# Transposing transfers from tile 12 on instead of tile 15, 12 load buffers instead of 18, and another place for the loads in the queue

## The chip, the cores and the metric

The kernel runs on one core of one Trainium2 chip. The metric is the time of one execution on the device, in microseconds (us); lower is better. The engines that matter are TensorE (PE, matrix products and transposes), VectorE (DVE), ScalarE (ACT), GpSimd (POOL, which here mostly issues loads) and SyncE (SP, which here issues transfers). Each of them works through its own instructions strictly in the order in which the program was written, and waits on semaphores where an operand isn't there.

## The reference

Chunked attention with memory slots, followed by a gated feed-forward network over all tokens. `q`, `k` and `v` are 4 batches x 8 heads x 768 positions x 64; each batch and head has 8 memory keys and values.

```python
chunk, left_ctx, right_ctx = (32, 16, 8)
for c in range(S // chunk):
    l_start, r_end = max(0, c*chunk - left_ctx), min(S, (c+1)*chunk + right_ctx)
    k_full = concat([mem_k, k[:, :, l_start:r_end]]); v_full = concat([mem_v, v[:, :, l_start:r_end]])
    a = softmax(scale * q_c @ k_full.T)
    out[:, :, c*chunk:(c+1)*chunk] = a @ v_full
x = out.transpose(0, 2, 1, 3).reshape(3072, 512)
return (relu(x @ w_gate) * (x @ w_val)) @ w_out        # 512 -> 1536 -> 512
```

## The kernel before

**Tiles and blocks.** The 3072 tokens are 24 tiles of 128 tokens, six to a batch: tiles 0 to 5 are batch 0, 6 to 11 batch 1, 12 to 17 batch 2, 18 to 23 batch 3. Attention is done tile by tile. The feed-forward network is done in eight blocks of `BLOCKS = [2, 2, 2, 4, 4, 4, 4, 2]` tiles, so block 3 holds tiles 6 to 9, block 4 tiles 10 to 13, block 5 tiles 14 to 17, block 6 tiles 18 to 21 and block 7 the last two. A block runs `first` (L407, products with `w_gate` and `w_val` into `g_ps` and `v_ps`, then ReLU on ACT, L413, and the gating product on DVE, L419) and then `second` (L432, the product with `w_out` into `out_ps`, copied and stored).

**One tile's attention**, with the keys of the operations in the program's own list of them (`ops`), `a` the tile and `i` 0 for q and 1 for k:

- `("qk", a, i)`: POOL loads q or k of the tile into a buffer of `ldpool` (L254), cast to bf16. There are 18 such buffers; the six v tiles of batch 0 come first and use them too.
- `("t", a, i)`, `("tc", a, i)`: the tile is transposed. For tiles 6 to 14 PE does it with four transposes into PSUM (L275), and ACT or DVE copies the result into `qT` or `kT`. For tiles from `LATE_QK` = 15 on, SP issues a transposing transfer from SBUF to SBUF (L283): q goes straight into `qT`, k into a buffer `k_t` (three of them) that ACT or DVE copies into `kT`. (Batch 0 has a way of its own, L236.)
- `("s", a)`: 32 small products give the scores (L309). Those of a tile also need the k of the next tile of its batch.
- `max`, `sub`, `exp`, `sum`, `rec`, `nrm`: the softmax, five operations on DVE (L322 to L352) and the exponent on ACT. Its result is `p_n`.
- `("p", a)`, `("pc", a)`: the probabilities P are transposed into `pT`, with four transposes on PE (L358) and a copy, or from tile `LATE_P` = 15 on by a transposing transfer of SP (L362).
- `("v", a)`: the value products (L388; L381 in batch 0) with `v_bd`, and `("x", a)`: the copy into `xT`, which the block's `first` reads.

`v_bd` has two copies: `v_bd[0]` serves batches 0 and 2, `v_bd[1]` batches 1 and 3. For batches 1 to 3, POOL loads v into it (`("vl", b, n)` and `("ve", b, n)`, L185, four issues), copies the memory rows into it (`("mr", b, n)`, L168, eight issues; for batch 1 SP does that), and ACT or DVE copies rows up inside it (`("up", ...)`). Batch 2's load waits until `v_bd[0]` has been zeroed after tile 5's values; batch 3's waits for tile 11's values.

**The order of the work** is written out ahead by a planner, `schedule()`. It has a list of operations with an assumed duration, dependencies (each with an assumed delay, where a number stands beside it), a priority and buffers to take and give (`room`), and steps through time: whenever an engine is free, it gets the ready operation of the best priority. Attention goes before feed-forward products, which fill the rest. The planner's times are assumptions only; what stays of them in the program is the order on each engine, and on the chip the semaphores decide. Of the constants: `ISSUE` is SP's time for one transposing transfer, `LAND` and `LAND_P` the time from there until its result is taken as there (q and k; P), `MARGIN` = 1.0 is added for attention products on PE. `pace(a)` holds PE's transposes of a tile back until a mark in the feed-forward work, `LEAD` = 31 us of it ahead of the block's start and 5.2 us later for each further tile; `pace_t(a)` holds SP's transfers of q and k back until the scores of an earlier tile have been put in the order. POOL's loads go in the order in which they were listed: `late` lists q and k of tiles 6 to 23, two a tile, k first; its first five stand ahead of `w_out`, and the loop over the batches lists each batch's v and memory rows and then a slice of `late`.

Of the kernel before, what the change touches and what calls it, by code (L numbers as in the profile page):

```python
# [19 lines left out]
def kernel(  # L20
# [24 lines left out]
    NT = B * TPB  # L45
# [7 lines left out]
    BAND0 = 48  # L53
    UT = 3

    LATE_QK, LATE_P = 15, 15

    KEY_RUNS = ((0, CH, 0), (KW, 64, CH), (CH, KW, CTX))
    assert sum(BLOCKS) == NT and NMEM == 8 and D == 64 and H == 8

    const = ctx.enter_context(tc.tile_pool(name="const", bufs=1))
    ldpool = ctx.enter_context(tc.tile_pool(name="ldpool", bufs=18))
    kvpool = ctx.enter_context(tc.tile_pool(name="kvpool", bufs=2))
    smpool = ctx.enter_context(tc.tile_pool(name="smpool", bufs=2))
    xtpool = ctx.enter_context(tc.tile_pool(name="xtpool", bufs=2))
# [294 lines left out]
    def p_transfer(a):  # L360
        PT[a] = smpool.tile([128, HP, 128], F16, name="pT", bufs=6)
        nc.sync.dma_start(PT[a], P_n.pop(a).rearrange("p h a s -> p (h a s)"), transpose=True)  # L362
# [72 lines left out]
    def store(blk, t, c, eng):  # L435
# [6 lines left out]
    starts = [sum(BLOCKS[:i]) for i in range(len(BLOCKS))]  # L442
# [3 lines left out]

    ops, loads = {}, []
    room = {"aps": 2, "sps": 1, "fps": 4, "mx": 2, "dif": 2, "p": 2, "sm": 2, "rinv": 2, "pn": 3, "kt": 3, "pT": 6,
            "qk": 18, "xT": 2, "gv": 2, "gr": 3, "o": 3, "kv": 2}

    def op(key, eng, fn, deps=(), prio=(0,), take=(), give=(), after=()):
        ops[key] = dict(eng=eng, fn=fn, deps=list(deps), prio=prio, take=list(take), give=list(give),
                        after=list(after))
# [42 lines left out]
    LEAD, STEP, AHEAD = 31.0, 5.2, 10.0  # L496
    marks, clock, begun = [], 0.0, {}
# [9 lines left out]

    def pace(a):
        blk = block_of[a]
        at = begun[blk] - LEAD + STEP * (a - starts[blk]) - (AHEAD if a >= LATE_P else 0.0)  # L510
        gone = [key for c, key in marks if c <= at]
        return gone[-1:] if blk >= 2 else []


    ISSUE, LAND, SLACK, LAND_P = 1.4, 4.5, 1.0, 3.0

    def pace_t(a):
        return [("s", a - 6)]

    for a in range(NT):  # L520
        b, t = divmod(a, TPB)
        last = t == TPB - 1
        for i in (1, 0):
            if b == 0:
                if t % 2 == 0:
                    for j in range(2):
                        op(("t", a + j, i), {"PE": 0.3}, lambda e, a=a, i=i, j=j: pair_t(a // 2, i, j),
                           [("pl", a // 2, i), "ib", ("new", b)], (1, a - i, -2 + j), ["aps"])
                        op(("tc", a + j, i), psum16(HP * 128) if t else {("ACT", "DVE")[j]: psum16(HP * 128)[("ACT", "DVE")[j]]}, lambda e, a=a, i=i, j=j: pair_copy(a // 2, i, j, engine[e]),
                           [("t", a + j, i)], (1, a - i, -2 + j), (), ["aps"])  # L530
                continue
            if a >= LATE_QK:
                op(("t", a, i), {"SP": ISSUE}, lambda e, a=a, i=i: qk_transfer(a, i),
                   [(("qk", a, i), SLACK), ("new", b)],
                   (1, a - i, 0), ["kt"] if i else [], [("qk", LAND)], pace_t(a))
                if i:
                    op(("tc", a, i), {"DVE": (0.2, 0.29), "ACT": (0.52, 0.62)}, lambda e, a=a, i=i: qk_copy(a, i, engine[e]),
                       [(("t", a, i), LAND)], (1, a - i, 0), (), ["kt"])
                continue
            op(("t", a, i), {"PE": 0.24}, lambda e, a=a, i=i: qk_t(a, i), [("qk", a, i), "ib", ("new", b)],  # L540
               (1, a - i, 0), ["aps"], ["qk"], pace(max(a - i, 0)))
            op(("tc", a, i), psum16(HP * 128), lambda e, a=a, i=i: qk_copy(a, i, engine[e]), [("t", a, i)],
               (1, a - i, 0), (), ["aps"])
        op(("s", a), {"PE": 0.36}, lambda e, a=a: scores(a),
           [(("t", a, 0), LAND) if a >= LATE_QK else ("tc", a, 0), ("tc", a, 1)]
           + ([] if last else [("tc", a + 1, 1)] if b or t % 2 == 0 else [("tc", a + 1, 1), ("tc", a + 2, 1)])
           + ([("tc", a ^ 1, 0)] if b == 0 else []), (1, a, 1), ["sps"],
           ["kv"] if last else [], [("s", a - 1)] if a else [])
        op(("max", a), {"DVE": (0.6 + (0.15 if t == 0 or last else 0), 0.7 + (0.15 if t == 0 or last else 0))}, lambda e, a=a: row_max(a), [("s", a)],
           (1, a, 2), ["mx"])  # L550
        op(("sub", a), {"DVE": (0.6, 0.69)}, lambda e, a=a: subtract(a), [("max", a)],
           (1, a, 3), ["dif"], ["sps", "mx"])
        op(("exp", a), {"ACT": (0.72, 0.83)}, lambda e, a=a: exponent(a), [("sub", a)], (1, a, 4), ["p"], ["dif"])
        op(("sum", a), {"DVE": (0.6, 0.69)}, lambda e, a=a: row_sum(a), [("exp", a)], (1, a, 5), ["sm"])
        op(("rec", a), {"DVE": (0.12, 0.2)}, lambda e, a=a: reciprocal(a), [("sum", a)], (1, a, 6), ["rinv"], ["sm"])
        op(("nrm", a), {"DVE": (0.6, 0.7)}, lambda e, a=a: normalise(a), [("rec", a)], (1, a, 7), ["pn"], ["p", "rinv"])
        if a < LATE_P:
            op(("p", a), {"PE": 0.24}, lambda e, a=a: p_t(a), [("nrm", a)], (1, a, 8), ["aps"], ["pn"])
            op(("pc", a), psum16(HP * 128), lambda e, a=a: p_copy(a, engine[e]), [("p", a)], (1, a, 9), ["pT"], ["aps"])
        else:  # L560
            op(("pc", a), {"SP": ISSUE}, lambda e, a=a: p_transfer(a), [("nrm", a)], (0, a), ["pT"], [("pn", LAND_P)])
        if b == 0:
            for c0 in (4 * t, 4 * t + 2):
                need = {c // 4 for c in (c0, c0 + 1)} | {max(c0 - 1, 0) // 4, min(c0 + 2, NCH - 1) // 4}
                gone = ([t - 1] if c0 % 4 == 0 and t else []) + ([t] if c0 == NCH - 2 else [])
                op(("sh", c0), {"PE": 0.4}, lambda e, c0=c0: shift(c0), [("vn", n) for n in sorted(need)] + ["ident"],
                   (1, a, 7.5), ["fps"], ["qk"] * len(gone), [("s", t)])
                op(("shc", c0), {"ACT": psum(2 * HP * D)["ACT"]} if t < 2 else psum(2 * HP * D), lambda e, c0=c0: shift_copy(c0, engine[e]), [("sh", c0)],
                   (1, a, 7.6), (), ["fps"])
        blk = block_of[a]  # L570
        j = a - starts[blk]
        op(("v", a), {"PE": 0.45 if b else 1.0}, lambda e, a=a: values(a),
           [("pc", a) if a < LATE_P else (("pc", a), LAND_P)]
           + ([("vl", b, n) for n in range(2)] + [("up", b, n, m) for n in range(2 * HP) for m in range(t // UT + 1)]
              + [("ve", b, n) for n in range(2) if last] if b else [("shc", 4 * t), ("shc", 4 * t + 2), "vm0"])
           + ([("mr", b, n) for n in range(2 * HP)] if b else []), (1, a, 10), ["aps"] + (["xT"] if j == 0 else []), ["pT"],
           [("v", a - 1)] if a else [])
        op(("x", a), psum(HP * 128), lambda e, a=a: x_copy(a, engine[e]), [("v", a)], (1, a, 11), (), ["aps"],
           [("x", a - 1)] if a else [])


    for rank, (blk, m) in enumerate(seq):
# [11 lines left out]
        else:  # L594
            last = None
            for t, c in [(t, c) for t in range(n) for c in pieces(blk, t)]:
                for m0 in range(0, NDC, MS):
                    end = (t, c, m0) == (n - 1, pieces(blk, t)[-1], NDC - MS)
                    op(("o", blk, t, c, m0), {"PE": MS * 0.000422 * (c[1] - c[0])},
                       lambda e, blk=blk, t=t, c=c, m0=m0: second(blk, t, c, m0),  # L600
# [5 lines left out]
                   lambda e, blk=blk, t=t, c=c: store(blk, t, c, engine[e]), [last], (0.5, rank), ["o"],  # L606
# [55 lines left out]
    for b in range(1, B):  # L662
        deps = ([("z0", hp, c0) for hp in range(HP) for c0 in range(0, NCH, 8)] if b > 1 else [("z1", hp) for hp in range(HP)]) + ([("v", TPB * (b - NSET + 1) - 1)] if b > NSET else [])
        if b == 1:
            for n in range(2 * HP):
                op(("mr", b, n), {"SP": 0.72}, lambda e, n=n: mem_rows(nc.sync, 1, n),
                   deps + [(("vm", 0), 0.2), (("vm", 1), 0.2)], (0,))
        for par in range(2):
            load_v_op(b, par, deps)
        if b > 1:  # L670
            for n in range(2 * HP):
                load(("mr", b, n), 192, 0.22, lambda b=b, n=n: mem_rows(nc.gpsimd, b, n),
                     deps + [(("vm", 0), 0.2), (("vm", 1), 0.2)])
        for a, i in late[5 if b == 1 else 9 + 12 * (b - 1):21 + 12 * (b - 1)]:
            load_qk_op(a, i)

    WARM = 18.0
# [4 lines left out]
    def schedule():  # L682
# [31 lines left out]
        while len(started) < len(ops) + len(loads):  # L714
# [8 lines left out]
            while moved:  # L723
                moved = False
                for e in ("POOL", "PE", "ACT", "DVE", "SP"):
# [18 lines left out]
                    else:  # L744
# [22 lines left out]
                        done[key] = end + 0.25 if e == "PE" else t + lat + 0.08  # L767

                        if queue_end > t:
                            queue_end += 1.1 if e == "SP" and key[0] in ("t", "pc") else 0.7 if key[0] == "oc" else 0.0  # L770
                        fn = lambda o=o, e=e: o["fn"](e)
                        for g in o["give"]:
                            g, lag = g if isinstance(g, tuple) else (g, 0.0)
# [49 lines left out]
```

## Time and profile before

| | |
|---|---|
| Time, median of 3 runs | 244.71 us (244.63 to 244.9) |
| The profiled execution | 244.74 us, its span 242.7 us |
| PE, DVE, ACT, POOL busy | 97%, 61%, 56%, 32% of the span |
| Granted TensorE clock, mean | 0.998 |
| DMA packets | 96413, 25.17 MB |
| Feed-forward blocks 2, 3, 4, 5, 6, 7 begin on PE | 66.9, 85.7, 122.4, 160.0, 192.6, 223.7 us |
| Scores of tiles 12, 13, 14 | 101.4, 109.9, 126.2 us |

The span runs from the first to the last instruction; the rest of the execution's time lies around it. All times below are us from the span's start unless said otherwise. In the groups by shape a line reads: source line, engine, operation, what is written and read, shapes, how many, then busy us and mean ns of one, then the engine's idle time just before them. In a timeline it reads: start, length, engine, line, operation, tiles, shapes, how many, and in brackets the idle time before it and what ended that; a sequencer that only issues has a q behind its engine's name. In the waits it reads: who, whom it waited for, us in total, how many times, the longest. In the DMA view a queue's line gives packets, MB, and the time its packets took as a share of 16 engines' time in the stretch asked for; several queues together can come to over 100%. q0 is POOL's queue, q1 SP's, q10 ACT's.

### The profile page before, as it was taken

What the parts mean: (1) busy time and instruction counts of PE and PEld (TensorE: products, weight loads), DVE (VectorE), ACT (ScalarE), POOL (GpSimd) and SP (SyncE); (2) the same over time, 40 slices, a digit from 0 to 9 for tenths busy, and PEclk for the clock granted to TensorE, in tenths of its full rate; (3) what the DMA queues carried; (4) which work ended last, traced back from release to release, by engine and by line L of the source; (5) the groups of instructions that cost most, each with busy time, mean ns of one, the idle gap of its engine ahead of it and who ended that gap; (6) DMA issues with size and microseconds to landing.
All of it is one profiled execution on the core that took longest, in us unless ns stands there. A gap on an engine that the chain in (4) does not pass through costs nothing.

```text
span 242.7 us, 6546 instructions
## 1 busy us (share of the span) xinstructions
PE 235.8 (97%) x2706; PEld 140.8 (58%) x2706; DVE 147.9 (61%) x296; ACT 136.0 (56%) x288; POOL 77.9 (32%) x102
## 2 busy tenths in 40 slices
PE   7898999999999999999999999999999999999994
PEld 5587887884589545554544545554445444445873
DVE  6674876988877458977549999894431043410430
ACT  7477777767885499665756674453332233312432
POOL 8975689235984396037430000000000000000000
PEclk9999999999999999999999999999999999999999
DMA  6999999999999999999990142651001210012102
GB/s 72 172 179 203 201 164 172 193 131 134 191 195 154 80 168 136 120 124 153 116 218 7 36 53 48 131 133 24 0 0 46 86 43 0 3 43 86 43 3 86
DMA packets 96413, 25.17 MB, mean 104 GB/s; under 512 B 87424, under 2 KB 93312, under 8 KB 96384
## 3 DMA queue, kind: packets, MB, share of 16 engines
q0 software_dynamic: 76128, 14.65, 83.5%
q1 hardware_dynamic: 16656, 3.82, 15.0%
q10 hardware_dynamic: 3600, 6.29, 8.1%
q8 instruction: 21, 0.34, 0.7%
q14 instruction: 8, 0.07, 0.1%
HBM read 28.55 MB, written 6.29 MB: 144 GB/s over the span
## 4 chain that ended last, share of the span: by engine, by line
PE 88%; ACT 4%; DMA 2%; POOL 2%; DVE 2%; issue 1%; ACTq 0%; POOLq 0%
PE v_ps L407 26%; PE g_ps L407 25%; PE out_ps L432 22%; PE xT_ps L388 3%; DMA v_n<-in_v_dram 2%; PE s_ps L309 2%; PE idle_ps L141 2%; PE vs_ps L215 2%; PE xT_ps L381 2%; PE pT_ps L358 2%; ACT v_bd L79 1%; PE qk_ps L275 1%; PE qk_ps L236 1%; POOL qk_p L227 1%; ACT o_sb L79 1%
## 5 line engine op out<-in xcount | busy, mean ns | idle before, releaser
L419 DVE TENSOR_TENSOR gvT<-v_ps,g_relu 128x256 f16<-128x256 f32 (+1 forms) x96 | 52.9, 554 | 58.2 <-PE v_ps L407 43.2
L407 PE MATMUL v_ps<-xT,w_val_sb 128*128 128x256 f16 (+1 forms) x384 | 78.2, 326 | 0.1
L407 PE MATMUL g_ps<-xT,w_gate_sb 128*128 128x256 f16 (+1 forms) x384 | 78.2, 326 | 0.0
L413 ACT ACTIVATE g_relu<-g_ps 128x256 f16<-128x256 f32 (+1 forms) x96 | 47.0, 491 | 47.6 <-PE g_ps L407 45.9
L432 PE MATMUL out_ps<-w_out_sb,gvT 128*128 128x512 f16 (+2 forms) x300 | 65.3, 371 | 0.0
L407 PEld LDWEIGHTS <-w_gate_sb 128*128 128x128 f16 x384 | 36.3, 98 | 23.1
L407 PEld LDWEIGHTS <-w_val_sb 128*128 128x128 f16 x384 | 36.0, 98 | 22.3 <-issue 0.5
L432 PEld LDWEIGHTS <-gvT 128*128 128x128 f16 x300 | 27.9, 98 | 29.9
L79 ACT COPY o_sb<-out_ps 128x512 f32<-128x512 f32 (+2 forms) x25 | 14.2, 567 | 31.8 <-PE out_ps L432 25.6
L337 ACT ACTIVATE p_exp<-dif 128x256 f16<-128x256 f32 (+2 forms) x72 | 19.6, 340 | 4.4 <-DVE dif L329 3.5
L322 DVE TENSOR_REDUCE mx<-s_ps 128x8 f32<-128x512 f32 x24 | 16.5, 688 | 5.6 <-PE s_ps L309 5.4
L341 DVE TENSOR_REDUCE sm<-p_exp 128x8 f32<-128x512 f16 x24 | 16.4, 683 | 4.4 <-ACT p_exp L337 4.1
L254 POOL DMA_DIRECT2D qk_b<-in_q_dram x18 | 16.4, 912 | 7.4 <-DMA v_bd<-in_v_dram 5.5
L254 POOL DMA_DIRECT2D qk_b<-in_k_dram x18 | 16.2, 903 | 5.5 <-DMA w_out_sb<-in_moe_w_out_dram 4.4
L79 ACT COPY v_bd<-v_bd 24x768 f16<-24x768 f16 (+1 forms) x20 | 15.6, 818 | 2.2 <-ACT o_sb L79 1.2
L352 DVE TENSOR_TENSOR p_n<-p_exp,rinv 128x512 f16<-128x512 f16 x24 | 16.5, 687 | 0.4
L329 DVE TENSOR_TENSOR dif<-s_ps,mx 128x512 f32<-128x512 f32 x24 | 16.4, 682 | 0.2
L185 POOL DMA_DIRECT2D v_bd<-in_v_dram x12 | 10.9, 920 | 12.5 <-PE v_ps L407 11.8
L168 POOL DMA_DIRECT2D v_bd<-vmem x16 | 10.5, 661 | 12.5 <-DMA v_bd<-in_v_dram 10.5
L79 ACT CAST xT<-xT_ps 128x512 f16<-128x512 f32 x17 | 9.9, 583 | 6.2 <-PE xT_ps L388 4.8
L141 PE MATMUL idle_ps<-idle 128*128 128x256 bf16 x69 | 11.5, 319 | 1.1 <-DVE warm L475 1.1
L388 PEld LDWEIGHTS <-v_bd 128*128 128x128 f16 x288 | 9.7, 96 | 3.2 <-issue 0.2
(57 smaller groups left out, 179.5 us busy)
## 6 DMA issues: line engine op xcount, KB each, us to landing
out_dram<-o_sb ACTq DMA_DIRECT2D x23, 256.0 KB
qk_b<-in_k_dram POOLq DMA_DIRECT2D x18, 128.0 KB, 7.2
qk_b<-in_q_dram POOLq DMA_DIRECT2D x18, 128.0 KB, 7.0
v_bd<-in_v_dram POOLq DMA_DIRECT2D x6, 384.0 KB, 11.5
w_out_sb<-in_moe_w_out_dram POOLq DMA_DIRECT2D x2, 768.0 KB, 10.5
qk_p<-in_k_dram POOLq DMA_DIRECT2D x3, 256.0 KB, 5.7
qk_p<-in_q_dram POOLq DMA_DIRECT2D x3, 256.0 KB, 6.6
v_n<-in_v_dram POOLq DMA_DIRECT2D x6, 128.0 KB, 6.5
```

The costliest lines, as they stand in the source:

```text
L79: nc.scalar.copy(o, i)
L254: nc.gpsimd.dma_start(qk_b[a, i], bass.AP(tensor=x.tensor, offset=x[b, 0, 128 * t, 0].offset, ap=[[D, 128], [S * D, H], [1, D]]))
L322: nc.vector.reduce_max(SM[a, "mx"], s4, axis=AX.X)
L329: nc.vector.tensor_tensor(out=SM[a, "dif"].rearrange("p (m r) a s -> p r m a s", r=2), in0=S_ps.pop(a).rearrange("p r (m a) s -> p r m a s ...
L337: nc.scalar.activation(p[:, :, :, s0:s0 + k1 - k0], dif[:, :, :, k0:k1], ACT.Exp, scale=SCALE)
L341: nc.vector.reduce_sum(SM[a, "sm"], SM[a, "p"], axis=AX.X)
L352: nc.vector.tensor_tensor(out=P_n[a], in0=SM.pop((a, "p")), in1=rinv_b, op=ALU.mult)
L388: nc.tensor.matmul(ps[:, hp, r], lhsT=v_bd[b % NSET][:, hp, 4 * t + g, :], rhs=x[:, hp, r], start=True, stop=True)
L407: nc.tensor.matmul(ps, lhsT=w[:, f, 128 * m:128 * m + 128], rhs=xTs[blk][:, f, :], start=(f == 0), stop=(f == NFC - 1))
L413: nc.scalar.activation(st["r", m], st.pop((0, m)), ACT.Relu)
L419: nc.vector.tensor_tensor(out=st["gv"][:, m, :], in0=st.pop((1, m)), in1=st.pop(("r", m)), op=ALU.mult)
L432: nc.tensor.matmul(st["o", t, c], lhsT=st["gv"][:, m, 128 * t:128 * t + 128], rhs=w_out_sb[:, m, c[0]:c[1]], start=(m == 0), stop=(m == ND ...
```

## The change

`LATE_QK` and `LATE_P` go from 15 to 12, so that q, k and P of tiles 12 to 14 are transposed by SP's transfers too. The load buffers go from 18 to 12. In the loads' order, seven loads of q and k (to the end of tile 11) stand behind batch 1's v, 21 (tile 12's k to tile 22's k) behind batch 2's v, and three behind batch 3's; before it was 16, 12 and three more. The planner's `LAND` goes from 4.5 to 7.5 us for tiles 12 and 13 and to 10 us from tile 14 on, `LAND_P` from 3.0 to 7.0 and 13.0 us, `ISSUE` from 1.4 to 1.5. SP's transfers of q and k may go once the scores of the tile four before, not six before, are in the order. PE's transposes of tiles 10 and 11 are held to 44 instead of 31 us ahead of block 4. The planner counts 1.5 instead of 1.1 us of POOL's queue for each of SP's transfers.

```diff
-    LATE_QK, LATE_P = 15, 15
+    LATE_QK, LATE_P = 12, 12
...
-    ldpool = ctx.enter_context(tc.tile_pool(name="ldpool", bufs=18))
+    ldpool = ctx.enter_context(tc.tile_pool(name="ldpool", bufs=12))
...
-            "qk": 18, "xT": 2, "gv": 2, "gr": 3, "o": 3, "kv": 2}
+            "qk": 12, "xT": 2, "gv": 2, "gr": 3, "o": 3, "kv": 2}
...
     def pace(a):
         blk = block_of[a]
-        at = begun[blk] - LEAD + STEP * (a - starts[blk]) - (AHEAD if a >= LATE_P else 0.0)
+        at = begun[blk] - (44 if blk >= 4 else LEAD) + STEP * (a - starts[blk]) - (AHEAD if a >= LATE_P else 0.0)
...
-    ISSUE, LAND, SLACK, LAND_P = 1.4, 4.5, 1.0, 3.0
+    ISSUE, SLACK = 1.5, 1.0
+    LAND = {a: 7.5 if a < 14 else 10.0 for a in range(NT)}
+    LAND_P = {a: 7.0 if a < 14 else 13.0 for a in range(NT)}
 
     def pace_t(a):
-        return [("s", a - 6)]
+        return [("s", a - 4)]
...
-                   (1, a - i, 0), ["kt"] if i else [], [("qk", LAND)], pace_t(a))
+                   (1, a - i, 0), ["kt"] if i else [], [("qk", LAND[a])], pace_t(a))
...
-            op(("pc", a), {"SP": ISSUE}, lambda e, a=a: p_transfer(a), [("nrm", a)], (0, a), ["pT"], [("pn", LAND_P)])
+            op(("pc", a), {"SP": ISSUE}, lambda e, a=a: p_transfer(a), [("nrm", a)], (0, a), ["pT"], [("pn", min(LAND_P[a], 7.0))])
...
-           [("pc", a) if a < LATE_P else (("pc", a), LAND_P)]
+           [("pc", a) if a < LATE_P else (("pc", a), LAND_P[a])]
...
-        for a, i in late[5 if b == 1 else 9 + 12 * (b - 1):21 + 12 * (b - 1)]:
+        for a, i in late[(5, 12, 33)[b - 1]:(12, 33, 36)[b - 1]]:
             load_qk_op(a, i)
...
-                            queue_end += 1.1 if e == "SP" and key[0] in ("t", "pc") else 0.7 if key[0] == "oc" else 0.0
+                            queue_end += 1.5 if e == "SP" and key[0] in ("t", "pc") else 0.7 if key[0] == "oc" else 0.0
```

(Two more lines put `LAND[a]` for `LAND` in the dependencies of the k copy and of the scores.)

More of the change, by code (lines that the diff above doesn't have):

```diff
@@ L534 @@
                    [(("qk", a, i), SLACK), ("new", b)],
-                   (1, a - i, 0), ["kt"] if i else [], [("qk", LAND)], pace_t(a))
+                   (1, a - i, 0), ["kt"] if i else [], [("qk", LAND[a])], pace_t(a))
                 if i:
                     op(("tc", a, i), {"DVE": (0.2, 0.29), "ACT": (0.52, 0.62)}, lambda e, a=a, i=i: qk_copy(a, i, engine[e]),
-                       [(("t", a, i), LAND)], (1, a - i, 0), (), ["kt"])
+                       [(("t", a, i), LAND[a])], (1, a - i, 0), (), ["kt"])
                 continue
@@ L544 @@
         op(("s", a), {"PE": 0.36}, lambda e, a=a: scores(a),
-           [(("t", a, 0), LAND) if a >= LATE_QK else ("tc", a, 0), ("tc", a, 1)]
+           [(("t", a, 0), LAND[a]) if a >= LATE_QK else ("tc", a, 0), ("tc", a, 1)]
            + ([] if last else [("tc", a + 1, 1)] if b or t % 2 == 0 else [("tc", a + 1, 1), ("tc", a + 2, 1)])
```

## The prediction

> **What bounds the kernel now.** I read the page first, then the waits of PE, the groups by shape, and the timelines of PE, SP and POOL with the DMA view for single stretches. The profiled execution took 244.74 us, of which 242.7 us are its span and 2.0 us lie around it; the median of the runs shown is 244.71 us, so a difference in the span can be taken off the median as it stands.
>
> ```profile
> span 242.7 us, 6546 instructions
> ...
> PE 235.8 (97%) x2706; PEld 140.8 (58%) x2706; DVE 147.9 (61%) x296; ACT 136.0 (56%) x288; POOL 77.9 (32%) x102
> ...
> PE   7898999999999999999999999999999999999994
> ...
> DVE  6674876988877458977549999894431043410430
> ...
> DMA  6999999999999999999990142651001210012102
> ```
>
> PE is full from the fourth slice on; the DMA engines are full up to slice 22 (about 133 us) as well, so two resources are near their end there. Do they hurt PE? Its own waits:
>
> ```profile
> PE idle_ps L141 <- DVE warm L475: 1.1, 1, 1.1
> PE qk_ps L236 <- DMA qk_p<-in_q_dram: 0.5, 1, 0.5
> PE vs_ps L215 <- DMA v_n<-in_v_dram: 0.5, 1, 0.5
> ```
>
> All three lie in the first 12 us, and for 85 to 124 us the same view is empty. So PE is the bound through its work, and work taken off PE is time, as long as no new wait comes.
>
> **What leaves PE.** Tiles 12, 13 and 14 give up their transposes on PE: 3 x (4 of q, 4 of k, 4 of the probabilities P) = 36 instructions.
>
> ```profile
> L358 PE MATMUL pT_ps<-band,p_n 128*128 128x128 f16 x60 | 5.8, 220 | 0.2 <-DVE qT L81 0.2
> L275 PE MATMUL qk_ps<-ident_b,qk_b 128*128 128x128 bf16 x72 | 5.8, 220 | 0.0
> ```
>
> 220 ns is the way of one through the pipeline, not its price. The price is read from where the next work starts:
>
> ```profile
> 92.50 0.61 PE L275 MATMUL qk_ps<-ident_b,qk_b 128*128 128x128 bf16 x8
> 92.94 1.03 PE L407 MATMUL v_ps<-xT,w_val_sb 128*128 128x512 f16 x4
> ...
> 115.95 0.39 PE L358 MATMUL pT_ps<-band,p_n 128*128 128x128 f16 x4
> 116.17 2.11 PE L432 MATMUL out_ps<-w_out_sb,gvT 128*128 128x512 f16 x9
> 118.12 0.56 PE L388 MATMUL xT_ps<-pT,v_bd 128*128 128x32 f16 x16
> 118.52 4.05 PE L432 MATMUL out_ps<-w_out_sb,gvT 128*128 128x512 f16 x18
> 122.40 1.03 PE L407 MATMUL g_ps<-xT,w_gate_sb 128*128 128x512 f16 x4
> ```
>
> Eight take 0.44 us and four take 0.22 us: 0.055 us each. 36 x 0.055 = 2.0 us, all on the path. With it go nine PSUM copies of 0.41 to 0.66 us on ACT or DVE, in place of which three k copies from SBUF come (0.28 us on DVE, 0.62 us on ACT); no engine but PE is on the path, so I count them at nothing.
>
> The Trainium skill (TensorE: Matmul & The Clock Gate, Part 4: PE-mode transpose) puts a transpose in a kernel at about 275 ns; the row's 220 ns is near that, its spacing of 55 ns is not, and by 275 ns the saving would be 9.9 us.
>
> **What is added.** Nine transposing transfers on SP's queue. Their two prices, from issues and packets:
>
> ```profile
> 71.98 1.31 SPq L283 DMA_TRANSPOSE k_t<-qk_b  x1
> 73.50 1.93 SPq L283 DMA_TRANSPOSE qT<-qk_b  x1
> 75.52 1.22 SPq L283 DMA_TRANSPOSE k_t<-qk_b  x1
> ```
>
> ```profile
> q1 hardware_dynamic: 1632, 0.39, 45.5%
> ```
>
> ```profile
> q1 hardware_dynamic: 544, 0.13, 31.3%
> ```
>
> The second fence is the DMA view from 71.98 to 83.7 us, the third from 136.57 to 138.65 us; a transfer is 544 packets. Alone, one that is issued at 136.57 has all its packets through by 138.65, 2.1 us later, and costs 0.313 x 2.08 = 0.65 us of 16 engines. Beside loads three cost 0.455 x 11.72 = 5.3 us, 1.8 each, and the last packets of the one issued at 75.52 start just before 83.7: up to 8.2 us from issue to end. So nine add 6 to 16 us of DMA packets to full stretches, and 9 x 1.2 to 1.9 = 11 to 17 us to SP's queue. Nothing of it is on the path while the score and value products find their operands there. On SP, a P transfer waits for its normalisation and holds back the q and k transfers queued behind it.
>
> The cover is the new distance. The order written out allows 1.5 + 7.5 us from the issue of q and k of tiles 12 and 13, 1.5 + 10 from tile 14 on, and 1.5 + 7 for P of 12 and 13, before 1.0 us of margin: 9 to 11.5 us against a worst 8.2 us seen. If the cover is gone, each late operand stops PE by the excess; before, only 1.4 + 4.5 were allowed and PE still did not wait, since those transfers were issued far ahead.
>
> **What is moved.** POOL's queue, before:
>
> ```profile
> 58.73 0.91 POOL L254 DMA_DIRECT2D qk_b<-in_k_dram  x1
> ...
> 67.46 3.80 POOL L185 DMA_DIRECT2D v_bd<-in_v_dram  x4 [0.52 <-DVE p_n L352]
> ...
> 84.26 0.92 POOL L254 DMA_DIRECT2D qk_b<-in_q_dram  x1
> ```
>
> 58.73 is the load of tile 12's k. It now stands behind batch 2's v (four issues) and eight memory-row copies. These can go at 58.73, since the last zeroing of that buffer on DVE ended at 55.6 us. They took POOL from 67.46 to 84.26, 16.8 us, so tile 12's k is issued at about 75.5 and lands near 80 (the load at 84.26 took 4.4 us). Tile 14's k, four loads of 0.9 us later, is issued at 79 and with 7 us lands at 86. Its transfer, issued near 88, is counted on by the order 11.5 us later; with a copy of 0.6 and the margin of 1.0 tile 13's scores come at about 101, where they stood at 109.9 before. They can, because tiles 10 and 11 are led by 44 instead of 31 us of feed-forward work, so their transposes move from 86 to about 73 us.
>
> The 12 load buffers bite from the 13th of these loads (tile 18's k), which waits for the transfer of tile 12's k; the last one ahead of batch 3's v waits for tile 16's k, which goes after tile 12's scores, at about 105. Batch 3's v was issued at 107.0 before, because of tile 11's values, and isn't used until 154. This I cost at nothing; its cover is some 30 us.
>
> Tiles 10 and 11 bring 2 x 3 us of softmax to DVE between 67 and 85 us; DVE was busy for 17.6 of the 25 us from 60 to 85, and 23.5 of 25 is tight. The nearest row is 30 to 60 us, with the same small blocks: DVE 24.9 of 30 and PE still 29.9 of 30. The wait in question is the 0.2 us in the row of L358, a P transpose that waited for a copy on DVE. The two tiles bring ten products to this stretch (four transposes of q and k, two each of scores, P and values). The bounds are -0.2 (that one wait vanishes) and +1.0 (half of the ten wait as long); I take +0.3, near the row of 30 to 60 us, which lost 0.1.
>
> **Sum.** -2.0 + 0.3 = -1.7 us, 244.7 - 1.7 = 243.0 us. The likeliest case's own range is 242.3 to 244.1.
>
> **Rivals.** (1) Slower: block 4 (tiles 10 to 13) starts late. Its first product stands at 122.40 and needs tile 13's xT; 28 of the 36 transposes lie ahead of it, so PE comes there at about 120.9. If tile 13's scores stay at 109.9 us, because its loads or transfers come late, its normalised P is ready at 114.6; 8.2 us of transfer, 0.6 of values and 0.7 of copy give 124.1. PE has nothing else to do and waits 3.2 us: 244.7 - 2.0 + 3.2 = 245.9 us. It decides from the point where tile 13's scores come after about 107; my estimate of 101 leaves 6 us. For it speaks that the DMA engines are full exactly there. The Trainium skill (DMA: Bandwidth & Descriptors, Issuing engines are not separate DMA queues) says that transfers of all issuers share the same 16 engines and interleave; 0.65 us alone against 1.8 beside loads agrees. Chance 0.21.
> (2) No change: score products of tiles 12 to 17 find single operands late, as SP falls behind its 1.5 us a transfer (7 steps from the issue at 88.63 to that at 101.72 took 1.9 us each, 0.4 more than counted). Over five waits of 0.3 to 0.4 us this eats the gain: 244.7 us. Chance 0.08.
> (3) Much faster: a transpose blocks PE for its 220 ns: 36 x 0.22 = 7.9, 236.8 us. The spacing speaks against it; by the skill's 275 ns it would be 234.8 us. Chance 0.01.
>
> **How the numbers follow.** The forecast has 0.70. Runs of this kernel tell 0.2%, 0.5 us, from no change. Faster by more: 0.71 (forecast and (3)); same 0.08; slower 0.21. The range goes from 242.0 (the full 2.0 us, the 0.2 us wait gone too, and 0.5 us of what a run can tell) to 246.0, where the first rival ends; later waits beyond that I put at 1 in 10.
>
> **What would show it.** PE's matmuls fall by 36, L275 from 72 to 48 and L358 from 60 to 48; SP's transposing transfers rise from 27 to 36. The L407 product of block 4 starts before 121.5 us and PE's waits stay empty after 60 us. Tile 13's scores near 101 us show the moved part right. Wrong it would be if PE's timeline has a gap ahead of block 4's first product, or waits of line 309 or 388 on a DMA.

## The result and the profile after

The changed kernel is slower: 252.59 us median (250.51 to 254.54, six runs) against 244.78 us (244.5 to 245.39, six runs), a ratio of 1.0301 with a 95% interval of 1.0262 to 1.0339 (the ratio leaves out the slowest of the six, 254.54 us, which is more than 1.5% above the fastest). The forecast was 243.0 us, between 242.0 and 246.0, so it was wrong, in sign as well as in size. The execution profiled took 252.97 us, its span 251.2 us: 8.5 us more span than before.

The page of the changed kernel, in the lines that answer to those shown of before, and the granted clock:

```profile
span 251.2 us, 6479 instructions
...
PE 237.8 (95%) x2670; PEld 139.8 (56%) x2670; DVE 148.2 (59%) x293; ACT 136.1 (54%) x285; POOL 77.4 (31%) x102
...
PE   7998999999999999999819999999999999999994
...
PEclk9999999999999999999976999999999999999999
```

The 36 instructions are gone from PE (2706 to 2670), and the groups by shape put them where they were expected:

```profile
L358 PE MATMUL pT_ps<-band,p_n 128*128 128x128 f16 x48 | 4.7, 220 | 0.2 <-DVE qT L81 0.2
L275 PE MATMUL qk_ps<-ident_b,qk_b 128*128 128x128 bf16 x48 | 4.0, 219 | 0.0
```

Yet PE is busy for 2.0 us longer. Two of its slices are no longer full, the 20th and 21st (119 to 132 us), and in the second of them and the one behind it the granted clock reads 0.7 and 0.6. PE's waits name one culprit that was not in the list before:

```profile
PE s_ps L309 <- ACT kT L79: 6.6, 2, 6.4
```

PE's timeline shows where it sits, in the middle of the scores of tile 18:

```profile
123.40 1.03 PE L407 MATMUL g_ps<-xT,w_gate_sb 128*128 128x512 f16 x4
124.36 0.21 PE L309 MATMUL s_ps<-kT,qT 64*32 64x48 bf16 x6
131.02 0.40 PE L309 MATMUL s_ps<-kT,qT 64*32 64x64 bf16 x26 [6.45 <-ACT kT L79]
131.35 1.89 PE L407 MATMUL v_ps<-xT,w_val_sb 128*128 128x512 f16 x4
```

Six of the 32 products run; the other 26 need the `kT` of the next tile, 19, which ACT copies from `k_t`. Behind the wait, four feed-forward products take 1.89 us instead of 1.03. ACT's timeline (ACTq is its sequencer, which issues the stores of the output) tells why the copy was late:

```profile
122.10 0.81 ACT L337 ACTIVATE p_exp<-dif 128x256 f16<-128x256 f32 x3 [3.25 <-DMA qT<-qk_b]
122.82 0.56 ACT L79 COPY o_sb<-out_ps 128x512 f32<-128x512 f32 x1
129.97 0.34 ACTq L439 DMA_DIRECT2D out_dram<-o_sb  x1
130.35 0.62 ACT L79 COPY kT<-k_t 128x512 bf16<-128x512 bf16 x1 [6.97 <-DMA k_t<-qk_b]
```

Read it from below. The copy at 130.35 stands behind the store at 129.97, and that store's data had been in `o_sb` since 123.4 (122.82 + 0.56). The releaser in the bracket is a transfer into `k_t`, but not the one that this copy reads: tile 19's k was issued on SP at 111.08 and had landed at 120.31. The chain of waits says which one it was:

```profile
114.81 0.48 ACT o_sb L79
115.28 14.62 DMA k_t<-qk_b
...
129.92 0.02 ACTq L439
...
130.35 0.63 ACT kT L79
...
131.02 0.40 PE s_ps L309 x21
```

The transfer issued at 115.28 is tile 20's k, whose result ACT does not need yet. It landed after 14.6 us, and what it released is the store (L439). The trace's semaphore events explain the connection: SP's transposing transfers and ACT's stores report their landing in turn on the same eight semaphores, and an issue waits until the DMA eight places ahead of it in that row has landed. Tile 20's k reports on semaphore 116 and was complete on it at 129.90; ahead of the store at 129.97, ACT's sequencer waits on the same semaphore 116, until 129.92. The store's place was that of tile 20's k. The first line of ACT's timeline has the same sign: an exponent reads nothing of `qT`, and was held for 3.25 us because the store ahead of it, at 121.71, waited for the place of a transfer of q (semaphore 114; issued at 112.45, landed at 121.64). These two stores went 2.87 and 6.59 us after the end of their copies. In the kernel before, none went later than 0.3 us.

Then the clock, from the windows of 122 to 128 us (in the wait) and 131.35 to 136.3 us (behind it). The columns are the stretch and its length, busy us and instructions of PE, PEld, DVE, ACT and POOL, the granted clock, the DMA share and GB/s:

```profile
122.00:128.00 6.00, 2.58 (x18) 0.99 (x16) 1.58 (x3) 1.28 (x4) 0.00 (x0) 1.00 1.31 116
131.35:136.30 4.95, 4.95 (x20) 1.76 (x14) 2.34 (x5) 2.00 (x6) 0.91 (x2) 0.52 1.94 174
```

4.95 us at 0.52 lose 4.95 x 0.48 = 2.4 us. With this the difference in span nearly adds up: -2.0 for the transposes (as predicted; the experiments below come near it), +6.45 of waiting at line 309, +2.4 of half clock, +0.5 between 75.95 and 77.44 us where a ReLU on ACT is late, +0.55 because the first feed-forward product starts at 23.77 instead of 23.21 us, +0.4 at the very end: 8.3 of 8.5 us. The 0.55 is scatter by all signs: the same product starts anywhere between 23.0 and 23.8 us in the other kernels' traces, at 23.77 in c2 too, which is the kernel before with later work edited.

### The profile page after: what moved, and what is told of

It is laid out like the page before. It is cut to its first block, busy times and chain, and to the rows that moved or that the text cites. A ratio compares the mean times of both kernels' runs of the same rounds, so it can differ in the third digit from the quotient of the medians.

```text
span 251.2 us, 6479 instructions
## 1 busy us (share of the span) xinstructions
PE 237.8 (95%) x2670; PEld 139.8 (56%) x2670; DVE 148.2 (59%) x293; ACT 136.1 (54%) x285; POOL 77.4 (31%) x102
## 4 chain that ended last, share of the span: by engine, by line
PE 81%; DMA 7%; ACT 7%; DVE 2%; issue 1%; ACTq 1%; SPq 0%
PE v_ps L407 25%; PE g_ps L407 24%; PE out_ps L432 18%; DMA k_t<-qk_b 6%; PE idle_ps L141 3%; PE xT_ps L388 2%; PE s_ps L309 2%; ACT v_bd L79 2%; PE qk_ps L236 2%; PE vs_ps L215 2%; PE xT_ps L381 1%; PE pT_ps L358 1%; DMA kmem_f<-in_mem_k_dram 1%; ACT p_exp L337 1%; ACT kT L79 1%
## 5 line engine op out<-in xcount | busy, mean ns | idle before, releaser
L407 PE MATMUL v_ps<-xT,w_val_sb 128*128 128x256 f16 (+1 forms) x384 | 79.7, 330 | 0.4 <-ACT g_relu L413 0.2
L407 PE MATMUL g_ps<-xT,w_gate_sb 128*128 128x256 f16 (+1 forms) x384 | 79.0, 329 | 0.0
L79 ACT COPY v_bd<-v_bd 24x768 f16<-24x768 f16 (+1 forms) x25 | 20.1, 820 | 1.7 <-ACT o_sb L79 1.2
L168 POOL DMA_DIRECT2D v_bd<-vmem x16 | 10.1, 643 | 17.8 <-DMA v_bd<-in_v_dram 17.5
L309 PE MATMUL s_ps<-kT,qT 64*32 64x64 bf16 (+2 forms) x768 | 7.9, 193 | 6.7 <-ACT kT L79 6.6
L141 PE MATMUL idle_ps<-idle 128*128 128x256 bf16 x69 | 12.1, 330 | 1.1 <-DVE warm L475 1.1
L309 PEld LDWEIGHTS <-qT 64*32 64x32 bf16 x768 | 4.9, 89 | 14.3 <-issue 13.7
L81 DVE CAST xT<-xT_ps 128x512 f16<-128x512 f32 x11 | 7.5, 680 | 8.9 <-PE xT_ps L388 8.9
```

The costliest lines, as they stand in the source:

```text
L79: nc.scalar.copy(o, i)
L141: nc.tensor.matmul(TMP["idle"][:, 0:N], lhsT=idle[:, 0:128], rhs=idle[:, 0:N], start=True, stop=True)
L309: nc.tensor.matmul(s[CH * g:CH * g + CH, r, o0:o0 + hi - lo], lhsT=qT[b][d, h2, CH * c:CH * c + CH], rhs=keys[d, h2, lo:hi], start=True, s ...
L407: nc.tensor.matmul(ps, lhsT=w[:, f, 128 * m:128 * m + 128], rhs=xTs[blk][:, f, :], start=(f == 0), stop=(f == NFC - 1))
```

## The experiments

Two theories. **A**: the stores on ACT wait for places that SP's transfers hold, and since ACT works in order, whatever stands behind a store waits too. **B**: the transfers are simply late, because the DMA engines are crowded at 110 to 130 us by batch 3's v and memory rows; whichever engine issues the stores, PE waits. All edits are to the changed kernel unless it says otherwise; "before" in a ratio is the kernel before, run beside it on the same chip.

| label | what differs | median us | ratio to before (95%) |
|---|---|---|---|
| e1_stores_sp | stores issued by SP | 245.74 | 1.0044 (1.0017 to 1.0072) |
| e2_kcopy_dve | k copies of late tiles on DVE | 250.33 | 1.0217 (1.0166 to 1.0268) |
| e3_no_mem3 | batch 3's memory rows left out | 247.4 | 1.012 (1.0065 to 1.0176) |
| e8_sp_nomem3 | e1 and e3 together | 242.66 | 0.9914 (0.9889 to 0.994) |
| e7_late15 | no additional transfers | 245.82 | 1.0056 (1.0042 to 1.0071) |
| e6_tr_old_loads | loads in the old place, 18 buffers | 248.37 | 1.0154 (1.0136 to 1.0172) |
| e5_late12_only | before, with only the two constants | 254.1 | 1.0374 (1.0332 to 1.0416) |
| c1_before_stores_sp | before, stores issued by SP | 245.01 | 1.0016 (0.9997 to 1.0035) |
| n1_sp_rows_late | e1, and batch 3's memory rows later | 242.83 | 0.9929 (0.9906 to 0.9952) |
| n2_sp_rows_old_loads | n1, loads in the old place, 18 buffers | 248.83 | 1.0165 (1.0142 to 1.0188) |
| n3_rows_late | the memory rows later, stores on ACT | 246.66 | 1.0102 (1.0069 to 1.0135) |
| c2_before_both | before, with n1's two edits | 245.72 | 1.0048 (1.003 to 1.0066) |

**The stores away from ACT.**

```diff
-        nc.scalar.dma_start(out[row:row + 128, c[0]:c[1]], o)
+        nc.sync.dma_start(out[row:row + 128, c[0]:c[1]], o)
```

> The changed kernel, with the output stores issued by SP instead of ACT, at the same places of the written-out order; nothing else differs. Theory A (shared slots): the transfers of SP and the stores of ACT take turns on the same eight semaphores, so a store cannot be issued before the transfer eight places ahead of it has landed; the store after the copy at 122.8 us waited until 129.9 for the k transfer issued at 115.3, and tile 19's k copy stood behind it on ACT while PE waited for that copy. With the stores on SP, ACT is not held: PE's wait at line 309 falls from 6.6 us to under 1 us, the granted clock shows no dip, and the time is 252.6 - 6.4 - 2.3 = 243.9 us (243 to 245). Theory B (late operands): the transfers themselves land after PE wants them, whoever issues the stores: the wait stays at 5 us or more and the time at 250 to 253 us.

245.74 us: 6.85 us of the loss are gone, by an edit that only moves the stores' issues from one engine to the other. That is 0.7 us above the range expected of theory A. PE's waits and ACT's timeline of this kernel show what is left:

```profile
PE s_ps L309 <- ACT kT L79: 2.2, 1, 2.2
```

```profile
134.95 0.62 ACT L79 COPY kT<-k_t 128x512 bf16<-128x512 bf16 x1 [4.63 <-DMA k_t<-qk_b]
```

The bracket looks like the one before, but here the transfer is the one that the copy reads: issued at 120.42, landed at 134.93, 14.5 us. So the 6.4 us wait was theory A's, and a smaller one of 2.2 us is theory B's.

**The copy away from ACT instead.**

```diff
-            copy(eng,
+            copy(nc.vector if a >= LATE_QK else eng,
```

> The changed kernel, with the k copies of the transferred tiles all on DVE, at the same places of the order. Theory A: PE's wait for tile 19's k copy goes, since DVE is not held by a store; but the ReLU stands behind the same store on ACT until about 130 us, and with four PSUM buffers PE can go on for two pairs of products (3.4 us) only. So a wait of about 3 us comes on the ReLU in place of 6.4 us on the copy, and the time is 247 to 250.5 us. Theory B: the copy has to wait for its transfer on DVE just as long; 6 us at line 309, 250 to 253 us.

250.33 us, which lies where the two ranges meet; the waits decide. Tile 18's scores now run at 124.00 us in one go, as the copy no longer stands behind the store. But the store still blocks ACT, and PE's timeline shows who stands behind it next:

```profile
128.45 1.02 PE L407 MATMUL v_ps<-xT,w_val_sb 128*128 128x512 f16 x4 [2.30 <-ACT o_sb L79]
131.01 1.87 PE L407 MATMUL g_ps<-xT,w_gate_sb 128*128 128x512 f16 x4 [1.54 <-ACT g_relu L413]
```

The output copies and the ReLU take the place of the k copy. This is A's mechanism seen from its other side: the store was the cause, and not the copy.

**The crowd on the DMA engines.** Batch 3's eight copies of memory rows (`mem_rows`, L168, eight partitions each) are left out.

```diff
-                load(("mr", b, n), 192, 0.22, lambda b=b, n=n: mem_rows(nc.gpsimd, b, n),
+                load(("mr", b, n), 192, 0.22, lambda b=b, n=n: None if b == 3 else mem_rows(nc.gpsimd, b, n),
```

> The changed kernel without the eight copies of batch 3's memory rows into v_bd (batch 3 then uses batch 1's memory values; the order of everything else is kept). It asks why the k transfer that was issued at 115.3 us took 14.6 us to land. Theory A with the rows as the clog: each of these copies works on eight partitions alone and the DMA engines moved little while they were in flight (122 to 128 us); without them that transfer lands within 10 us, the store's slot is free by 125, PE waits under 2 us, 244 to 247 us. Theory A with the number of transfers and batch 3's v as the clog: the transfer still takes over 12 us, 250 to 253 us. Theory B says the same as the latter.

247.4 us, 0.4 us above the range in which the rows are the clog, and 2.6 below the other. Tile 20's k, now issued at 115.56, lands in 8.7 us instead of 14.6: without these eight small copies its landing is 5.9 us shorter. PE still waits 1.8 us for a ReLU, 0.9 for a k copy and 0.6 for the softmax, as the stores still share the places (three of them stood for 2.9, 1.0 and 3.3 us); the clock of the profiled execution stays at 1.00.

**Both taken away.** e8_sp_nomem3 has the edits of the first and the third experiment.

> The changed kernel with the stores on SP and without batch 3's memory rows (batch 3 then uses batch 1's memory values). With the stores on SP alone one wait of 2.2 us was left, on the k transfer issued at 120.4 us, which took 14.5 us to land; without the rows the same place took 8.7 us with the stores on ACT. If these two are all there is, no wait over 0.5 us is left after 80 us, the clock shows no dip, and the gain of the 36 transposes is seen at last: 242.7 to 243.5 us. If the eight slots or the DMA engines are full anyway, the transfer still lands 12 us or more after its issue and the time is 245 to 247 us.

242.66 us, 1.8 us below the kernel before beside it (244.44 us), with no wait of PE over 0.3 us behind 80 us. In the window of 122 to 128 us PE is busy for all 6.00 us, with 66 instructions in the place of 18.

Each of the two causes alone costs: with the stores moved and the rows left, 245.74; with the rows gone and the stores left, 247.4; with neither, a gain near the 2.0 us of the transposes appears in the time.

**The rearrangement without the transfers.**

```diff
-    LATE_QK, LATE_P = 12, 12
+    LATE_QK, LATE_P = 15, 15
```

> The changed kernel without its extra transfers: tiles 12 to 14 go back to PE, all else (place of the loads, 12 buffers, distances, pace of four tiles) stays. If the nine extra transfers fill the slots, the wait is gone and the time is that of the kernel before, 244 to 245.5 us. If the pace of four tiles, which moves the transfers of tiles 16 to 21 back into the stretch of batch 3's v, is enough by itself, a wait of 2 us or more stays: 246.5 to 253 us.

245.82 us, 0.3 above the first range, without a long wait (the longest behind 60 us is 0.65 us, at line 309 for the softmax). Two transfers still took 12.4 and 11.4 us (issued at 103.68 and 105.16), but without the nine additional ones no store stood for over 0.3 us. The rest of the rearrangement costs about 1.4 us by itself (244.44 us beside it), of which the profile shows 0.65 as one wait. What the remainder is, and which part of the rearrangement brings it, was not assigned.

**The transfers without parts of the rearrangement.** e6_tr_old_loads undoes the place of the loads, e5_late12_only is the kernel before with the two constants.

```diff
-    ldpool = ctx.enter_context(tc.tile_pool(name="ldpool", bufs=12))
+    ldpool = ctx.enter_context(tc.tile_pool(name="ldpool", bufs=18))
...
-            "qk": 12, "xT": 2, "gv": 2, "gr": 3, "o": 3, "kv": 2}
+            "qk": 18, "xT": 2, "gv": 2, "gr": 3, "o": 3, "kv": 2}
...
-        for a, i in late[(5, 12, 33)[b - 1]:(12, 33, 36)[b - 1]]:
+        for a, i in late[5 if b == 1 else 9 + 12 * (b - 1):21 + 12 * (b - 1)]:
```

> Transfers from tile 12 on, with the new distances and paces, but with the old place of the loads and 18 buffers. If the place of the loads or the 12 buffers bring the stall (batch 3's v loads fall into the thickest transfers because of them), it is gone: 242.5 to 245 us. If it is the number and the pace of the transfers against eight shared slots, a wait of ACT's stores on a transfer and then of PE of over 2 us stays somewhere, 246 to 253 us.

```diff
-    LATE_QK, LATE_P = 15, 15
+    LATE_QK, LATE_P = 12, 12
```

> The kernel before with one part of the change: tiles 12 to 14 transposed by transfers; the distances, the pace, the buffers and the place of the loads stay. Theory A, with the thick stretch of transfers at batch 3's v as its cause: the transfers run six tiles ahead here, so fewer fall beside that load, and 242.5 to 244.5 us come out, unless the short distance of P (3 us counted, where landings beside loads took 5 to 9) makes PE wait at the values of tiles 12 to 14: three waits of 1 to 4 us, 246 to 252 us, named as line 388 waiting for a P transfer.

248.37 us, with five waits of 0.2 to 1.5 us at line 309, and 254.1 us, more than the whole change costs and above both of its ranges.

e6 has the mechanism of its second expectation, but no wait of PE over 2 us. ACT's timeline:

```profile
125.60 0.82 ACT L337 ACTIVATE p_exp<-dif 128x256 f16<-128x256 f32 x3 [5.91 <-DMA k_t<-qk_b]
```

This exponent stands behind a store issued at 125.20, 5.5 us after its data was there: its place was that of a k transfer issued at 112.66, which took 12.5 us. The softmax on DVE was held by the exponent, and PE's waits of 0.22 and 1.46 us follow at 128.5 and 130.2 us.

PE's waits of e5, and then one line of its ACT timeline:

```profile
PE xT_ps L388 <- DMA pT<-p_n: 5.4, 2, 3.7
PE v_ps L407 <- ACT o_sb L79: 2.6, 1, 2.6
```

```profile
88.46 2.29 ACT L79 COPY v_bd<-v_bd 24x768 f16<-24x768 f16 x3 [4.67 <-DMA v_bd<-in_v_dram]
```

The first wait is what the longer `LAND_P` is for: P transfers that are counted on too early (they took 7.5 and 12.5 us from issue to landing, and 1.4 + 3.0 were counted). The changed kernel has no wait at line 388; since e5 lacks the other parts of the rearrangement too, that the distance alone removes it is not shown. The second wait is not due to a store without a place; no store of this kernel stood. The copy into `o_sb` is queued on ACT behind copies inside `v_bd`, and these stood for batch 2's v, whose load was issued at 70.29, behind the loads of q and k in the old place, and landed at 88.44.

**The control.** c1_before_stores_sp is the first edit made to the kernel before.

> A control: the kernel before, with the output stores issued by SP. Its stores never waited long for a slot on ACT, so by theory A (a store on ACT waits for the landing of a transfer eight places ahead) nothing is to be gained here: 244.3 to 245.0 us. If stores on SP are better by themselves (ACT saves about 0.3 us an issue, or the last store ends sooner), it is 243 to 244, and that much has to be taken off what the same edit did to the changed kernel.

245.01 us, a ratio whose interval holds 1. So stores on SP are no gain in the kernel before, where no store had to wait.

**A version without either cause that computes all.** n1_sp_rows_late has the stores on SP, and lets SP copy batch 3's memory rows after the scores of tile 20 in the planner's order. On the chip SP issues them between 132.2 and 137.9 us, the last lands at 141.5, and the values of tile 18, the first to use them, come at 146.4 us (at 154.6 in the kernel before).

```diff
-         if b > 1:
+         if b == 3:
+             for n in range(2 * HP):
+                 op(("mr", b, n), {"SP": 0.72}, lambda e, b=b, n=n: mem_rows(nc.sync, b, n),
+                    deps + [("s", 20), (("vm", 0), 0.2), (("vm", 1), 0.2)], (0,))
+         elif b > 1:
```

(The values of batch 3 count on a row 5.0 us after its issue.)

> The changed kernel with the stores on SP, and batch 3's memory rows copied by SP after the scores of tile 20 in the order, instead of by POOL right behind batch 3's v (the values of tile 18 are counted on 5 us later). The whole computation is there. If the shared slots and these rows are all that cost time, it comes out as the kernel without the rows did, with no wait over 0.5 us after 80 us: 242.3 to 243.0 us, 0.8% under the kernel before. If the rows clog wherever they lie, or hold SP's queue, a wait of 1 us or more comes at 140 to 170 us: 243.5 to 246 us.

242.83 us (242.21 to 244.09, six runs): 0.7% faster than the kernel before (0.5 to 0.9%), and the fastest of the kernels that do the whole work. Its page:

```profile
span 240.6 us, 6496 instructions
...
PE 233.6 (97%) x2670; PEld 138.4 (58%) x2670; DVE 147.6 (61%) x293; ACT 136.5 (57%) x285; POOL 72.5 (30%) x94
```

The span is 2.1 us under that of before, PE is busy for 2.2 us less, and tile 18's scores run in one go, from 123.04 us on. (The profiled execution took 242.33 us, 0.5 us less than the median.)

**What of n1 is needed.** n2 is n1 with the loads in the old place and 18 buffers (e6's edit), n3 is n1 with the stores left on ACT, c2 is the kernel before with n1's two edits.

> The same with the old place of the loads and 18 buffers, which took 248.4 us with the stores on ACT and the rows on POOL. If the place of the loads costs nothing once slots and rows are out of the way: 242.3 to 243.5 us. If the old place is worse by itself (batch 2's v late, many transfers queued behind late loads), a part of the 4 us stays: 244 to 248 us.

> The changed kernel with batch 3's memory rows late, and the stores on ACT as they were. If the shared slots hurt by themselves, also where no transfer takes 14 us (all of them took 7 to 10 us without the rows), ACT still waits 2 to 4 us on a slot now and then, and PE behind it: 245.5 to 248 us, as the kernel without the rows. If the slots only hurt by the one late transfer: 242.5 to 244 us.

> A control for the version with the stores on SP and batch 3's memory rows late: the same two edits in the kernel before, which keeps its 36 transposes on PE. If the gain there (0.7% under the kernel before) is that of the transposes, this one stays within 0.2% of the kernel before, 244.2 to 245.4 us. If the two edits gain by themselves, it is below 244 us.

n2 takes 248.83 us. Batch 2's v now stands behind the loads of q and k, while tiles 10 and 11 come earlier. PE waits twice for a `pT` copy on DVE, 4.5 us in all and 3.7 us at the longest. The timeline of DVE there:

```profile
88.95 0.62 DVE L81 COPY v_bd<-v_bd 24x768 f16<-24x768 f16 x2 [5.28 <-DMA v_bd<-in_v_dram]
89.60 0.42 DVE L81 COPY pT<-pT_ps 128x512 f16<-128x512 f16 x1
```

DVE stands for 5.3 us before a copy of v whose load is late; the `pT` copy that PE needs is queued behind it. So the loads' new place, "behind batch 2's v", is a needed part and no mere neighbour of the transfers. (The 18 buffers came back with the old place; the bracket names the load.) n3 takes 246.66 us: in the profiled execution (245.6 us) 1.3 us of PE's time go to a ReLU behind a store on ACT, so the shared places cost by themselves, though less when the transfers land in time (10.4 us at most). c2 takes 245.72 us, 1.1 us more than the kernel before beside it (244.61 us) and above both of its ranges: PE waits 1.2 us for a `pT` copy on ACT, queued behind a k copy that stood 2.66 us for its transfer. So the two edits are worth something with the change only.

## Why the prediction was wrong

**Right: what leaves PE.** The counts came as predicted, and the price of 0.055 us each agrees with the two kernels that have no long wait: n1 has 2.1 us less span than before, e8 242.7 - 240.8 = 1.9 us, against 2.0 predicted. No run takes the transposes away and nothing else, so the agreement of the size may be luck in part.

**Misread, without effect.** The prediction has the DMA engines full up to slice 22 (133 us) and PE full from the fourth slice; the rows of the page say slice 21 (127 us) and the fifth. No term rests on it.

**Right: what is moved.** Tile 12's k was issued at 74.27 us (75.5 predicted) and landed at 77.77 (80); tile 14's landed at 85.09 (86) and its transfer went at 85.11 (88). Tile 13's scores came at 100.99, predicted at about 101, and so rival 1, which needed them after 107, did not come: block 4's first product at 123.40 (the line above) has no wait ahead of it. It is later than the 121.5 us named as the sign, in part because the scores of tiles 14 to 17 (about 0.24 us each) now lie ahead of it, in part by the 0.55 and 0.5 us lost earlier; this sign was badly chosen. Batch 3's v was issued at 108.42 (107.0 before), near what was expected.

**Mis-sized, and on another engine: block 2.** 0.5 us were lost between 75.95 and 77.44 us, where 0.3 had been counted for DVE's softmax. PE's timeline names ACT:

```profile
77.44 0.60 PE L407 MATMUL v_ps<-xT,w_val_sb 128*128 128x256 f16 x4 [0.23 <-ACT g_relu L413]
```

That ReLU stood behind a copy inside `v_bd` on ACT (0.83 us from 76.15). Between 60 and 85 us DVE was busy for 21.3 of 25 us, less than the 23.5 feared, but ACT for 22.3, after 16.8 before: the earlier load of batch 2's v brings its copies there, which the prediction did not count. n1 has the same wait.

**Failed: "What is added", the cover and above all who waits on it.** Two errors, one in "9 to 11.5 us against a worst 8.2 us seen" and one in what follows it. First, 8.2 us was read from the last packets. By the semaphores the transfers issued at 73.50 and 75.52 in the kernel before landed at 85.04 and 85.24, after 11.5 and 9.7 us: the cover of 9 to 11.5 us was already used up by rows of the trace of before. Beside batch 3's v and the memory rows it became 14.6 us. This error did not stop the products of tile 18: the k that they read, tile 19's, had landed at 120.31, 4 us before they began. It shows in e1, where PE waits 2.2 us for a k that took 14.5 us. Second, and this is the 6.45 us, the step looked for who waits for a late transfer only among those who read it. "If the cover is gone, each late operand stops PE by the excess" puts the price of a late transfer at its own reader; in truth it went to a store on another engine, through a place in a row of eight, and from there to all that is queued on ACT. For that no bound was given, and none of the rivals had it: that "slower" had a chance of 0.21 rests on a late block 4, which did not come. With it went "no engine but PE is on the path": ACT is, as soon as its sequencer stands.

**Not counted: what a wait costs behind it.** The 6.45 us wait was followed by 2.4 us of half clock. The rivals priced waits at their length alone.

The part "What would show it" named waits of line 309 as a sign of error, on a DMA; it was line 309, on ACT.

**What stays open.** Why the memory-row copies hold up transfers so much. They are small, and the DMA engines move only 116 GB/s in the window of 122 to 128 us in which everything waits, while POOL stands for 10.13 us before the seventh copy of rows (at 128.03). POOL's issues have a row of eight semaphores of their own, and eight places ahead lies the third issue of batch 3's v, which took 17.5 us (110.23 to 127.75). SP issued eight transfers in that time. In the kernel before, the same issue took 9.7 us, with the same rows behind it and one transfer issued meanwhile; in e3, without the rows, it took 17.5 us again, with ten transfers issued meanwhile, though tile 20's k landed in 8.7. So the rows lengthen the transfers, and v takes longer where more transfers go beside it; why, no run shows. That the rows' eight partitions put the load on half of the DMA engines is a guess. The Trainium skill (DMA: Bandwidth & Descriptors, Why a DMA increments its semaphore by 16 and not by 1) says that the slowest dimension of a transfer sets how many engines it uses. No run here changed the rows' shape, so this is argued, and not shown.

## What to carry to other kernels

Before moving work to DMA transfers, list every DMA in flight with its issue and its landing by semaphore, and look for who waits for the place of a late one, not only for its data: an issue that can't go blocks the whole queue of its engine. Don't issue stores from an engine that also feeds the critical path, when another queue holds long transfers that share its places; where no place is short, as in the kernel before, moving them gained nothing. And when a late transfer comes to light, look at what small copies run beside it before adding distance.

## What the runs showed of the hardware that was not expected

- The same transposing transfer of 128 KB takes 2.4 us from issue to landing alone (issued at 136.57 us in the kernel before, landed at 139.0), 7.4 to 9.4 us with up to six DMAs of SP in flight (e8, between 78 and 131 us), and 14.6 us beside the memory rows.
- The releaser in a bracket can name a DMA that the instruction doesn't read. The sign is a compute instruction behind an issue on the same engine, like the exponent at 122.10 us "released" by a transfer into `qT`.
- The clock fell to about half for 3 to 7 us in or behind waits of PE of 6.45 us (the changed kernel), 2.2 us (e1), 2.3 + 1.5 us (e2), 3.66 us (n2, 0.54 from 90.1 to 93.8) and, in e5, 1.65 us (0.50 from 124.2 to 127.5) and 3.72 us (0.50 from 131.0 to 134.4), but not behind one of 2.6 us (e5), 1.8 us (e3) or 1.3 us (n3). So no single length decides here. The Trainium skill (TensorE: Matmul & The Clock Gate, Why this matters for your kernels) warns of idle gaps of more than about 3 us; the dips behind 2.2 and 1.65 us are below that.
- In these programs the DMAs of SP and ACT report on the same eight semaphores in turn (108, 111, 112, 114 to 118 in the trace of the changed kernel), those of POOL on eight others (99 to 106), and each issue waits for the landing eight places ahead in its row.
